# Moving an elementwise product from GpSimd to VectorE, pairing all down-projection blocks and placing two early chains anew, in a fused attention and bilinear-FFN kernel

## Chip, cores, metric

The kernel runs on one core of one Trainium2 chip. The metric is device time in microseconds (us) for one execution. Most executions of one kernel agree within 0.3%. Spans in the profile are 1.4 to 2 us shorter than the times, since they run from the first to the last instruction.

## The reference

Eight batches of eight heads attend to 32 memory slots. The result goes through a feed-forward layer that multiplies two projections.

```python
# q, k, v: (8, 8, 576, 64); phi: (8, 8, 576, 32)
a = softmax(phi, over the sequence)                 # written out in the reference
k_m = einsum('bhsm,bhsd->bhmd', a, k)
v_m = einsum('bhsm,bhsd->bhmd', a, v)
attn = softmax(q @ k_m^T / sqrt(64), over the 32 slots)
x = (attn @ v_m) as (4608, 512)                     # tokens x (heads * head_dim)
out = ((x @ w_a) * (x @ w_b)) @ w_out               # w_a, w_b: (512, 1536), w_out: (1536, 512)
```

## The kernel before

`attn @ v_m @ w_a` is computed as `attn @ (v_m @ w_a)`. So each batch has a **chain** (sums of k and v, transposes, scores, exponentials E, denominators, reciprocals R, the product A = E·R) and a **fold** of the weights (`vab`). They feed the **up-projections** (`pa`, `pb`, giving `ht`) and the **down-projections**. The chain of batch b+1 is cut into units that are laid, slot by slot, between the up-projections of batch b. An up-projection of 288 tokens takes two slots here. Some of the code, cuts marked:

```python
        def normalise(g, hfs=slice(0, 2)):                       # two per batch: g = 0, 1
            ...
            nc.scalar.activation(out=t["R", g][:, sl], in_=t["L", g][:, sl], func=AF.Exp, scale=-1.0)
            engine = nc.vector if b < 3 else nc.gpsimd           # <- the product of E and R
            engine.tensor_tensor(out=attn[b][:, g, sl], in0=t["E"][:, g, sl], in1=t["R", g][:, sl], op=ALU.mult)
```

The down-projections of two blocks of 128 tokens are done as one pair with seven products of half blocks in place of eight. That needs four sums of `ht` blocks per pair, on GpSimd. The second needs the first and the third needs the second. The fourth needs neither.

```python
    def sum_tokens(cidx, engine):
        ...
        for out, in0, in1, op in ((t[0], a21, a22, ALU.add), (t[1], t[0], a11, ALU.subtract),
                                  (t[2], a12, t[1], ALU.subtract), (t[3], a11, a21, ALU.subtract)):
            engine.tensor_tensor(out=out, in0=in0, in1=in1, op=op)
            yield
```

Of the 36 blocks, the first four are done early by themselves, thirty in fifteen pairs, block 34 by itself, and block 35 last, in two half-width accumulations (`last_down`).

A PSUM bank holds what the matmuls write until another engine has copied it out; this is called evacuating it. An up-projection evacuates its two banks by ScalarE (`a_sb`) and VectorE (`ht`). All PSUM tiles share eight banks, given out in the order of last use:

```python
        pa = banks.tile([P, HALF], F32, name="pa")
        ...                                                      # two matmuls of 288 columns
        nc.scalar.copy(out=a_sb, in_=pa)
        ...
        pb = banks.tile([P, HALF], F32, name="pb")
        ...                                                      # two matmuls
        nc.vector.tensor_tensor(out=ht[:, i, t0:t0 + HALF], in0=a_sbs[hf - hfs[0]], in1=pb, op=ALU.mult)
```

The order of the units is written as strings, one word per slot (`nr1` is the second product with its reciprocals, `qt` a transpose of q, `kv` and `km` the sums of k and v and their evacuation, a prime the batch after next):

```python
    every = "- sc+e0 e1 den0 v0+x0a+x0b - - nr0 exp0' - v1+x1a x1b+qt0' den1 - exp1' v2+x2a+x2b nr1+qt1' - kv'+km' qt2' kvt'+qt3' L - -"
```

The softmax here doesn't subtract the row's maximum and nothing guards it: scores larger than these inputs give would overflow.

Of the kernel before, what the change touches and what calls it, by code (L numbers as in the profile page):

```python
# [8 lines left out]
F32 = mybir.dt.float32  # L9
F16 = mybir.dt.float16  # L10
AF = mybir.ActivationFunctionType
ALU = mybir.AluOpType

P = 128
CS = 16.0
# [3 lines left out]
def kernel(  # L19
# [167 lines left out]
    def units(b):  # L187
# [129 lines left out]
        def normalise(g, hfs=slice(0, 2)):  # L317
            if g == 0 and hfs.start == 0:
                attn[b] = mid.tile([P, 2, S], F16, name="A")
            sl = slice(HALF * hfs.start, HALF * hfs.stop)  # L320
            if hfs.start == 0:
                t["R", g] = small.tile([P, S], F16, name="R")
            nc.scalar.activation(out=t["R", g][:, sl], in_=t["L", g][:, sl], func=AF.Exp, scale=-1.0)  # L323
            engine = nc.vector if b < 3 else nc.gpsimd
            engine.tensor_tensor(out=attn[b][:, g, sl], in0=t["E"][:, g, sl], in1=t["R", g][:, sl], op=ALU.mult)  # L325

        def fold(lo, hi, zs):
# [73 lines left out]
    def down(cidx):  # L401

        po, bank = banks.take([P, d_model], F32, "po", hold=True)
        yield from down_part(po, bank, cidx, 0, NFF)

    def last_down(cidx):

        pair, c = divmod(cidx, NI)
        w = d_model // 2
        for x in range(2):  # L410
            cs = slice(w * x, w * (x + 1))
            po = banks.tile([P, w], F32, name="pl")
            o_sb = opool.tile([P, w], F32, name="o_sb")
            for i in range(NFF):
                nc.tensor.matmul(po, ht[:, i, P * c:P * (c + 1)], wo_sb[:, i, cs],
                                 start=(i == 0), stop=(i == NFF - 1))
            nc.scalar.mul(out=o_sb[:, :w // 2], in_=po[:, :w // 2], mul=1.0 / (CS * CS))
            nc.vector.tensor_scalar(out=o_sb[:, w // 2:], in0=po[:, w // 2:], scalar1=1.0 / (CS * CS), scalar2=None,
                                    op0=ALU.mult)
            for z, engine in enumerate((nc.sync, nc.scalar)):  # L420
                slot = 2 * c + z
                engine.dma_start(out=out_rows[2 * pair + slot // NI, slot % NI, :, cs],
                                 in_=o_sb[64 * z:64 * z + 64, :])

    EARLY = 4

    def early_downs():
# [28 lines left out]
    def sum_tokens(cidx, engine):  # L456

        h_sums[cidx] = spool.tile([P, 4, KH, P], F16, name="h_sums")
        t = [h_sums[cidx][:, x] for x in range(4)]
        (a11, a12), (a21, a22) = ([tokens_of(cidx + y, x) for x in range(2)] for y in range(2))  # L460
        for out, in0, in1, op in ((t[0], a21, a22, ALU.add), (t[1], t[0], a11, ALU.subtract),
                                  (t[2], a12, t[1], ALU.subtract), (t[3], a11, a21, ALU.subtract)):
            engine.tensor_tensor(out=out, in0=in0, in1=in1, op=op)  # L463
            yield

    def store(o_sb, cidx):
        pair, c = divmod(cidx, NI)
        for z in range(2):
            slot = 2 * c + z
            nc.sync.dma_start(out=out_rows[2 * pair + slot // NI, slot % NI], in_=o_sb[64 * z:64 * z + 64, :])  # L470

    def two_downs(self, cidx):
        S1, S2, S4, S3 = (h_sums[cidx][:, x] for x in range(4))
        T1, T2, T3, T4 = (w_sums[:, x] for x in range(4))
        (a11, a12), (a21, a22) = ([tokens_of(cidx + y, x) for x in range(2)] for y in range(2))
        scale = 1.0 / (CS * CS)

        def products(po, lhs, rhs, first=False):
            for i in range(KH):
                nc.tensor.matmul(po, lhs[:, i], rhs[:, i], start=first and i == 0,  # L480
                                 stop=i == KH - 1, skip_group_check=not first)
                if i < KH - 1:
                    yield

        def part(po, name):
            x = ppool.tile([P, NH], F32, name=name)
            nc.scalar.mul(out=x, in_=po, mul=scale)
            return x

        def plus(o, po, x):  # L490
            nc.vector.scalar_tensor_tensor(out=o, in0=po, scalar=scale, in1=x, op0=ALU.mult, op1=ALU.add)

        o1, o2 = (opool.tile([P, d_model], F32, name="o_sb") for _ in range(2))
        y, ybank = banks.take([P, NH], F32, "py", hold=True)
        yield from products(y, a11, quarter(0, 0), True)
        u1 = part(y, "u1")
        yield
        v, vbank = banks.take([P, NH], F32, "pv", hold=True)
        self.brim = True
        yield from products(v, S1, T1, True)  # L500
        u5 = part(v, "u5")
        yield
        yield from products(y, S2, T2)
        u2 = part(y, "u2")
        yield
        yield from products(v, S4, quarter(1, 1))
        banks.free(vbank)
        plus(o1[:, NH:], v, u2)
        self.brim = False
        yield  # L510
        yield from products(y, S3, T3)
        plus(o2[:, NH:], y, u5)
        yield
        x, xbank = banks.take([P, NH], F32, "px", hold=True)
        self.brim = True
        yield from products(x, a12, quarter(1, 0), True)
        banks.free(xbank)
        plus(o1[:, :NH], x, u1)
        store(o1, cidx)
        self.brim = False  # L520
        yield
        yield from products(y, a22, T4)
        banks.free(ybank)
        nc.scalar.mul(out=o2[:, :NH], in_=y, mul=scale)
        store(o2, cidx + 1)
        yield

    BLOCKS = B // 2 * NI
    LEAD = 24
    PLAIN = 0  # L530
    PAIRED = range(EARLY + PLAIN, BLOCKS - 2, 2)

    class Work:

# [7 lines left out]
            self.next_sum = next(self.sums)  # L542

        def products(self):
            for cidx in range(EARLY, EARLY + PLAIN):
                yield from down(cidx)
            for cidx in PAIRED[:-1]:
                yield from two_downs(self, cidx)
            yield from down(BLOCKS - 2)
            yield from two_downs(self, PAIRED[-1])  # L550

        def add_up(self):
            for n, cidx in enumerate(PAIRED):
                for x in range(4):
                    yield n, NFF * PLAIN + 7 * KH * n + KH * (x + 1)
                    if x == 0:
                        sums = sum_tokens(cidx, nc.gpsimd if n < len(PAIRED) - 1 else nc.vector)
                    next(sums)
            while True:
                yield len(PAIRED), 0  # L560

# [21 lines left out]
        def plan(self, tokens, slots, keep=24):  # L583

            n = min(max(0, tokens // P - PAIRED[0]) // 2, len(PAIRED))
            self.summed = n
            self.ready = NFF * min(PLAIN, tokens // P - EARLY) + 7 * KH * n + NFF * (tokens // P >= BLOCKS - 1)
            self.rate = max(0, self.ready - self.done - keep) / slots
            self.owed = 0.0
            self.sum_ahead()  # L590
# [78 lines left out]
    def chain(b, plan):  # L669


        for x in plan.split():
# [4 lines left out]
            else:  # L677
# [2 lines left out]
    fill(16)  # L680
    chain(0, "exp0 exp1 ks0 f3 kt0 qt0 qt1 f14 s0 e0 ks1 f3 kt1 qt2 qt3 f6 den0 f4 s1 nr0 e1 f6 vs0 vs1 vt0 vt1 den1 f3 "
             "hv0a hx0a nr10 nr11 hv0b hx0b f4")
    ups(steps(0, 0, 4), slots(0, "- hv1a+hx1a - hv1b+hx1b - v1a+x1a - v1b+x1b"))
    load(2)
    ups(steps(0, 4, 12), slots(0, "- - - - v2a+x2a - v2b+x2b"))
    chain(1, "exp0 exp1 y9 ks0 y3 kt0 qt0 qt1 y1 ks1 y3 kt1 s0 e0 qt2 qt3 y6 den0 y2 s1 e1 nr0 y4 den1 y2 vs0 vs1 y1 vt0 vt1 nr1 y1 hv0a hx0a y2 hv0b hx0b y2")
    load(3)
    sum_weights()
    ups(steps(1, 0, 4), slots(1, "y1 hv1a+hx1a hv1b+hx1b y1 v1a+x1a v1b+x1b y3 y3"))
    ups(half_steps(1, 0, 4), slots(1, "- v2a+x2a+v2b+x2b+qt0' - exp0' - exp1'+qt1' - qt2'+kv'+km'+y9"))  # L690
    work.plan(S + HALF, 10)
    ups(half_steps(1, 1, 4), slots(2, "qt3 kvt - sc+e0+e1+den0 - nr0+den1+v0+x0a - - x0b+nr1 - v1+x1b+x1a -"))
    second = "v2_+x2a_+exp0 x2b_ - exp1 qt0+kv+km - qt1+kvt+qt2 qt3 sc+e0 - e1+v0+x0a x0b den0+v1+x1a nr0+L x1b+exp0' den1 - nr1+v2+x2a - x2b+exp1' qt0' kv'+qt1' km' - qt2'+kvt'+qt3'"
    every = "- sc+e0 e1 den0 v0+x0a+x0b - - nr0 exp0' - v1+x1a x1b+qt0' den1 - exp1' v2+x2a+x2b nr1+qt1' - kv'+km' qt2' kvt'+qt3' L - -"
    last = "sc+e0 - e1 - v0 x0b den1+x0a - den0 - nr0+v1+x1a nr1 x1b - - - - - - v2+x2a - - - x2b"
    for b in range(2, B):
        if b == 2:
            load(4)
# [4 lines left out]
            ups(half_steps(b, hf), side[NFF * hf:NFF * (hf + 1)] if hf == 0 else side[NFF:])  # L703
    work.plan(S * B, 1, 0)
    work.pull(work.ready - work.done)
    last_down(B // 2 * NI - 1)
# [1 line left out]
_INS = ['q', 'k', 'v', 'phi', 'moe_w_a', 'moe_w_b', 'moe_w_out']  # L708
_OUTS = [((4608, 512), 'float32')]
# [25 lines left out]
```

## Time and profile before

| | before |
|---|---|
| time, median of 3 | 247.81 us (247.73 to 247.85) |
| span of the profiled execution | 246.4 us |
| TensorE busy | 234.4 us, 95% |
| VectorE / ScalarE / GpSimd busy | 68% / 64% / 61% |

What bounds the kernel (TensorE) is shown in the prediction. Two more views of the kernel before matter for what follows. First, three groups of instructions by line. The columns are line, engine, operation, out<-in and count, then busy us and mean ns, then idle time of the engine just before and what ended it.

```profile
L612 PE MATMUL pb<-A,vab 128*128 128x288 f16 x384 | 76.5, 286 | 0.2
L463 POOL TENSOR_TENSOR h_sums<-ht 128x768 f16<-128x768 f16 x28 | 45.9, 1640 | 34.0 <-DVE ht L615 34.0
L325 POOL TENSOR_TENSOR A<-E,R 128x576 f16<-128x576 f16 x10 | 12.8, 1278 | 11.9 <-ACT R L323 11.6
```

Ten products on GpSimd take 1.28 us each, and the second half of each up-projection (`pb`) hardly waits: 0.2 us in 384 matmuls. Second, the timeline of GpSimd around one second product, of the sixth batch (columns: start, duration, engine, line, operation, tiles):

```profile
151.22 1.64 POOL L463 TENSOR_TENSOR h_sums<-ht,h_sums 128x768 f16<-128x768 f16 x1
152.92 1.28 POOL L325 TENSOR_TENSOR A<-E,R 128x576 f16<-128x576 f16 x1
154.15 1.64 POOL L463 TENSOR_TENSOR h_sums<-ht 128x768 f16<-128x768 f16 x1
```

GpSimd takes the third sum of a pair, then the product, then the fourth sum, without a pause. In the fourth, fifth and seventh batch, too, the second product stands between these two sums (at 100.60, 122.92 and 178.26).

### The profile page before, as it was taken

How to read it: one execution, taken by the hardware profiler on the slowest of the kernel's cores; microseconds unless marked ns; L12 is line 12 of the kernel's file. 1: busy time of each engine (PE TensorE's matmuls, PEld its weight loads, DVE VectorE, ACT ScalarE, POOL GpSimd, SP SyncE). 2: the span in 40 equal slices, each digit the busy share in tenths (PEclk: the TensorE clock that was granted, in tenths of full speed). 3: DMA queues.
4: the chain of work that ended last, by engine and by line, in shares of the span. 5: the costliest groups of instructions: out<-in, count | busy, mean ns of one | idle time of the engine just before them, and what ended most of it. 6: DMA issues, size and time to landing. Idle time of an engine off the chain costs nothing.

```text
span 246.4 us, 7681 instructions
## 1 busy us (share of the span) xinstructions
PE 234.4 (95%) x3049; PEld 167.1 (68%) x3049; DVE 166.5 (68%) x401; ACT 157.9 (64%) x409; POOL 151.1 (61%) x123
## 2 busy tenths in 40 slices
PE   7589999999998999999999999999999999999993
PEld 3354574456655857777787777877787787888782
DVE  3636794477959967876994649865995686756620
ACT  2247772578697489578856768588855877565330
POOL 8724233499799029892899759892849186936000
PEclk9999999999999999999999999999999999999999
DMA  6999999999979804973159732695120303033145
GB/s 198 210 198 206 211 252 207 255 220 271 233 183 207 160 4 108 238 127 85 33 149 208 174 85 45 167 207 145 32 56 3 88 7 82 10 78 71 43 104 128
DMA packets 26036, 33.82 MB, mean 137 GB/s; under 512 B 1936, under 2 KB 20368, under 8 KB 26000
## 3 DMA queue, kind: packets, MB, share of 16 engines
q0 software_dynamic: 19280, 22.71, 50.3%
q1 hardware_dynamic: 6288, 9.90, 16.3%
q10 hardware_dynamic: 432, 0.72, 0.8%
q8 instruction: 24, 0.39, 0.6%
q14 instruction: 12, 0.10, 0.1%
HBM read 42.47 MB, written 9.44 MB: 211 GB/s over the span
## 4 chain that ended last, share of the span: by engine, by line
PE 74%; DMA 17%; DVE 3%; POOL 2%; ACT 1%; issue 1%; ACTq 0%; DVEq 0%; POOLq 0%
PE pa L602 18%; PE pb L612 16%; PE py L480 15%; PE pv L480 8%; DMA phi_sb<-in_phi_dram 6%; DMA wo_sb<-in_moe_w_out_dram 6%; DMA wb_sb<-in_moe_w_b_dram 5%; PE pva L337 5%; PE px L480 4%; PE po L389 3%; PE pkv L213 2%; PE pD L314 1%; PE pscore L292 1%; PE pT L242 1%; POOL q_sb L90 1%
## 5 line engine op out<-in xcount | busy, mean ns | idle before, releaser
L615 DVE TENSOR_TENSOR ht<-a_sb,pb 128x288 f16<-128x288 f16 x192 | 82.9, 448 | 40.2 <-ACT a_sb L605 29.3
L605 ACT CAST a_sb<-pa 128x288 f16<-128x288 f32 x192 | 74.7, 405 | 31.6 <-PE pa L602 31.0
L602 PE MATMUL pa<-A,vab 128*128 128x288 f16 x384 | 76.5, 287 | 1.4 <-DVE A L325 1.4
L612 PE MATMUL pb<-A,vab 128*128 128x288 f16 x384 | 76.5, 286 | 0.2
L463 POOL TENSOR_TENSOR h_sums<-ht 128x768 f16<-128x768 f16 x28 | 45.9, 1640 | 34.0 <-DVE ht L615 34.0
L612 PEld LDWEIGHTS <-vab 128*128 128x128 f16 x384 | 37.0, 98 | 13.2 <-issue 1.9
L602 PEld LDWEIGHTS <-vab 128*128 128x128 f16 x384 | 34.5, 98 | 15.9 <-issue 9.1
L480 PEld LDWEIGHTS <-h_sums 128*128 128x128 f16 x360 | 35.1, 98 | 6.5 <-issue 0.4
L349 ACT CAST vab<-pva 128x512 f16<-128x512 f32 (+1 forms) x52 | 28.1, 558 | 10.0 <-PE pva L337 10.0
L349 DVE CAST vab<-pva 128x512 f16<-128x512 f32 (+1 forms) x52 | 32.8, 643 | 2.4 <-PE pva L337 2.0
L480 PEld LDWEIGHTS <-ht 128*128 128x128 f16 x270 | 26.4, 98 | 5.4 <-issue 0.2
L480 PE MATMUL py<-w_sums,h_sums 128*128 128x256 f16 x180 | 28.5, 272 | 0.0
L463 POOL TENSOR_TENSOR h_sums<-h_sums,ht 128x768 f16<-128x768 f16 x14 | 23.1, 1650 | 1.0
L463 POOL TENSOR_TENSOR h_sums<-ht,h_sums 128x768 f16<-128x768 f16 x14 | 23.0, 1642 | 1.0
L305 ACT ACTIVATE E<-pscore 128x288 f16<-128x288 f32 x32 | 11.4, 416 | 13.6 <-PE pscore L292 13.5
L325 POOL TENSOR_TENSOR A<-E,R 128x576 f16<-128x576 f16 x10 | 12.8, 1278 | 11.9 <-ACT R L323 11.6
L389 PE MATMUL po<-wo_sb,ht 128*128 128x512 f16 x60 | 16.0, 381 | 0.1
L480 PE MATMUL py<-wo_sb,ht 128*128 128x256 f16 x90 | 15.2, 273 | 0.0
L480 PE MATMUL pv<-w_sums,h_sums 128*128 128x256 f16 x90 | 15.2, 273 | 0.0
L204 DVE STREAM_TRANSPOSE qT<-q_sb 128x288 f32<-128x288 f32 x32 | 14.5, 463 | 0.6 <-DMA q_sb<-in_q_dram 0.6
L480 PE MATMUL py<-w_sums,ht 128*128 128x256 f16 x90 | 14.7, 272 | 0.1
L315 ACT ACTIVATE L<-pD 128x288 f32<-128x288 f32 x32 | 11.4, 413 | 5.0 <-PE pD L314 4.8
(66 smaller groups left out, 273.1 us busy)
## 6 DMA issues: line engine op xcount, KB each, us to landing
out_dram<-o_sb SPq DMA_DIRECT2D x70, 128.0 KB, 2.4
kv_sb<-in_v_dram POOLq DMA_DIRECT2D x7, 576.0 KB, 10.5
phi_sb<-in_phi_dram POOLq DMA_DIRECT2D x7, 576.0 KB, 4.6
kv_sb<-in_k_dram POOLq DMA_DIRECT2D x7, 576.0 KB, 8.2
q_sb<-in_q_dram POOLq DMA_DIRECT2D x6, 576.0 KB, 12.8
wo_sb<-in_moe_w_out_dram POOLq DMA_DIRECT2D x3, 512.0 KB, 17.4
q_sb<-in_q_dram POOLq DMA_DIRECT2D x4, 288.0 KB, 12.7
wa_sb<-in_moe_w_a_dram POOLq DMA_DIRECT2D x2, 512.0 KB, 14.8
```

The lines of the kernel that those rows point to most:

```text
L204: nc.vector.transpose(out=t["qT"][:, hp, :].bitcast(F32), in_=qs[b][:, hp, :].bitcast(F32))
L305: nc.scalar.activation(out=Ev[:, g, :, z, :], in_=pss, func=AF.Exp, scale=1.0 / (8.0 * CS))
L325: engine.tensor_tensor(out=attn[b][:, g, sl], in0=t["E"][:, g, sl], in1=t["R", g][:, sl], op=ALU.mult)
L337: nc.tensor.matmul(t["pva", lo, z][g][0][32 * j:32 * j + 32, 0:hi - lo], t["kvT"][64 * r:64 * r + 64, 4 + g, M * j:M * j + M], w_sbs[z][64 ...
L349: engine_copy(out=vabs[b][z][:, g, lo:hi], in_=pva[:, 0:hi - lo])
L389: nc.tensor.matmul(po, ht[:, i, P * c:P * (c + 1)], wo_sb[:, i, :], start=(i == 0), stop=(i == NFF - 1))
L463: engine.tensor_tensor(out=out, in0=in0, in1=in1, op=op)
L480: nc.tensor.matmul(po, lhs[:, i], rhs[:, i], start=first and i == 0, stop=i == KH - 1, skip_group_check=not first)
L602: nc.tensor.matmul(pa, vab[0][:, g, fs], A[:, g, HALF * hf:HALF * (hf + 1)], start=(g == 0), stop=(g == 1))
L605: nc.scalar.copy(out=a_sb, in_=pa)
L612: nc.tensor.matmul(pb, vab[1][:, g, fs], A[:, g, HALF * hf:HALF * (hf + 1)], start=(g == 0), stop=(g == 1))
L615: nc.vector.tensor_tensor(out=ht[:, i, t0:t0 + HALF], in0=a_sbs[hf - hfs[0]], in1=pb, op=ALU.mult)
```

## The change

By the diff, its intent is to take work off GpSimd, whose product takes 2.8 times as long as VectorE's (1.28 and 0.46 us), to do the last two blocks as a sixteenth pair, and to place units where TensorE waits less. The core of the diff, cuts marked:

```diff
-            engine = nc.vector if b < 3 else nc.gpsimd
+            engine = nc.vector
 ...
-    def last_down(cidx):
-        ...
-    def store(o_sb, cidx):
+    def store(o_sb, cidx, cs=slice(0, d_model), engines=(nc.sync, nc.sync)):
 ...                                  # the last pair stores its second block in two halves
-    PAIRED = range(EARLY + PLAIN, BLOCKS - 2, 2)
+    PAIRED = range(EARLY, BLOCKS, 2)
 ...
-                        sums = sum_tokens(cidx, nc.gpsimd if n < len(PAIRED) - 1 else nc.vector)
+                        sums = sum_tokens(cidx, nc.gpsimd if n < len(PAIRED) - 2 else nc.vector)
 ...                                  # first batch's folds, second batch's chain: five more lines
-    ups(steps(0, 0, 4), slots(0, "- hv1a+hx1a - hv1b+hx1b - v1a+x1a - v1b+x1b"))
+    ups(steps(0, 0, 4), slots(0, "hv1a+hv1b hx1b+hx1a - - - v1a+x1a v1b x1b"))
 ...                                  # later batches: second, every, last
-    every = "- sc+e0 e1 den0 v0+x0a+x0b - - nr0 exp0' - v1+x1a x1b+qt0' den1 - exp1' v2+x2a+x2b nr1+qt1' - kv'+km' qt2' kvt'+qt3' L - -"
+    every = "- sc+e0 e1 den0 v0+x0a+x0b - - nr0+exp0' - - v1+x1a qt0' x1b+den1 exp1' - v2+x2a+x2b nr1+qt1' kv'+km' qt2' - qt3' - kvt'+L -"
```

More of the change, by code (lines that the diff above doesn't have):

```diff
@@ L404, in down @@
         yield from down_part(po, bank, cidx, 0, NFF)
-    def last_down(cidx):
-        pair, c = divmod(cidx, NI)
-        w = d_model // 2
-        for x in range(2):
-            cs = slice(w * x, w * (x + 1))
-            po = banks.tile([P, w], F32, name="pl")
-            o_sb = opool.tile([P, w], F32, name="o_sb")
-            for i in range(NFF):
-                nc.tensor.matmul(po, ht[:, i, P * c:P * (c + 1)], wo_sb[:, i, cs],
-                                 start=(i == 0), stop=(i == NFF - 1))
-            nc.scalar.mul(out=o_sb[:, :w // 2], in_=po[:, :w // 2], mul=1.0 / (CS * CS))
-            nc.vector.tensor_scalar(out=o_sb[:, w // 2:], in0=po[:, w // 2:], scalar1=1.0 / (CS * CS), scalar2=None,
-                                    op0=ALU.mult)
-            for z, engine in enumerate((nc.sync, nc.scalar)):
-                slot = 2 * c + z
-                engine.dma_start(out=out_rows[2 * pair + slot // NI, slot % NI, :, cs],
-                                 in_=o_sb[64 * z:64 * z + 64, :])
     EARLY = 4
@@ L469, in store @@
             slot = 2 * c + z
-            nc.sync.dma_start(out=out_rows[2 * pair + slot // NI, slot % NI], in_=o_sb[64 * z:64 * z + 64, :])
+            engines[z].dma_start(out=out_rows[2 * pair + slot // NI, slot % NI, :, cs], in_=o_sb[64 * z:64 * z + 64, cs])
     def two_downs(self, cidx):
@@ L476, in two_downs @@
         scale = 1.0 / (CS * CS)
+        ends = cidx == PAIRED[-1]
         def products(po, lhs, rhs, first=False):
@@ L512, in two_downs @@
         plus(o2[:, NH:], y, u5)
+        if ends:
+            store(o2, cidx + 1, slice(NH, d_model))
         yield
@@ L524, in two_downs @@
         nc.scalar.mul(out=o2[:, :NH], in_=y, mul=scale)
-        store(o2, cidx + 1)
+        if ends:
+            store(o2, cidx + 1, slice(0, NH), (nc.sync, nc.scalar))
+        else:
+            store(o2, cidx + 1)
         yield
@@ L529 @@
     LEAD = 24
-    PLAIN = 0
-    PAIRED = range(EARLY + PLAIN, BLOCKS - 2, 2)
+    PAIRED = range(EARLY, BLOCKS, 2)
     class Work:
@@ L544, in products @@
         def products(self):
-            for cidx in range(EARLY, EARLY + PLAIN):
-                yield from down(cidx)
-            for cidx in PAIRED[:-1]:
+            for cidx in PAIRED:
                 yield from two_downs(self, cidx)
-            yield from down(BLOCKS - 2)
-            yield from two_downs(self, PAIRED[-1])
         def add_up(self):
@@ L554, in add_up @@
                 for x in range(4):
-                    yield n, NFF * PLAIN + 7 * KH * n + KH * (x + 1)
+                    yield n, 7 * KH * n + KH * (x + 1)
                     if x == 0:
-                        sums = sum_tokens(cidx, nc.gpsimd if n < len(PAIRED) - 1 else nc.vector)
+                        sums = sum_tokens(cidx, nc.gpsimd if n < len(PAIRED) - 2 else nc.vector)
                     next(sums)
@@ L586, in plan @@
             self.summed = n
-            self.ready = NFF * min(PLAIN, tokens // P - EARLY) + 7 * KH * n + NFF * (tokens // P >= BLOCKS - 1)
+            self.ready = 7 * KH * n
             self.rate = max(0, self.ready - self.done - keep) / slots
@@ L682 @@
              "hv0a hx0a nr10 nr11 hv0b hx0b f4")
-    ups(steps(0, 0, 4), slots(0, "- hv1a+hx1a - hv1b+hx1b - v1a+x1a - v1b+x1b"))
+    ups(steps(0, 0, 4), slots(0, "hv1a+hv1b hx1b+hx1a - - - v1a+x1a v1b x1b"))
     load(2)
-    ups(steps(0, 4, 12), slots(0, "- - - - v2a+x2a - v2b+x2b"))
-    chain(1, "exp0 exp1 y9 ks0 y3 kt0 qt0 qt1 y1 ks1 y3 kt1 s0 e0 qt2 qt3 y6 den0 y2 s1 e1 nr0 y4 den1 y2 vs0 vs1 y1 vt0 vt1 nr1 y1 hv0a hx0a y2 hv0b hx0b y2")
+    ups(steps(0, 4, 12), slots(0, "- - - - v2a+x2a+v2b+x2b - -"))
+    chain(1, "exp0 exp1 y9 ks0 y3 kt0 qt0 qt1 y1 y3 ks1 qt2 s0 e0 y6 kt1 qt3 den0 y3 s1 nr0 e1 y4 y2 den1 vs0 vs1 vt0 y1 vt1 nr1 hv0a hx0a hv0b y3 hx0b y2")
     load(3)
     sum_weights()
-    ups(steps(1, 0, 4), slots(1, "y1 hv1a+hx1a hv1b+hx1b y1 v1a+x1a v1b+x1b y3 y3"))
-    ups(half_steps(1, 0, 4), slots(1, "- v2a+x2a+v2b+x2b+qt0' - exp0' - exp1'+qt1' - qt2'+kv'+km'+y9"))
+    ups(steps(1, 0, 4), slots(1, "- hv1a+hx1a hv1b+hx1b+y1 - v1a+x1a y3+v1b x1b y3"))
+    ups(half_steps(1, 0, 4), slots(1, "- v2a+x2a+v2b+x2b+qt0' - - qt1'+exp0'+qt2' exp1' - kv'+km'+y9"))
     work.plan(S + HALF, 10)
-    ups(half_steps(1, 1, 4), slots(2, "qt3 kvt - sc+e0+e1+den0 - nr0+den1+v0+x0a - - x0b+nr1 - v1+x1b+x1a -"))
-    second = "v2_+x2a_+exp0 x2b_ - exp1 qt0+kv+km - qt1+kvt+qt2 qt3 sc+e0 - e1+v0+x0a x0b den0+v1+x1a nr0+L x1b+exp0' den1 - nr1+v2+x2a - x2b+exp1' qt0' kv'+qt1' km' - qt2'+kvt'+qt3'"
-    every = "- sc+e0 e1 den0 v0+x0a+x0b - - nr0 exp0' - v1+x1a x1b+qt0' den1 - exp1' v2+x2a+x2b nr1+qt1' - kv'+km' qt2' kvt'+qt3' L - -"
-    last = "sc+e0 - e1 - v0 x0b den1+x0a - den0 - nr0+v1+x1a nr1 x1b - - - - - - v2+x2a - - - x2b"
+    ups(half_steps(1, 1, 4), slots(2, "- kvt qt3 sc+e0+e1+den0 - nr0+den1+v0+x0a - - x0b+nr1 - v1+x1b x1a"))
+    second = "v2_+x2a_+exp0 x2b_ exp1 - qt0+kv+km - qt1+qt2 kvt+qt3 sc+e0 - e1+v0+x0a den0+x0b v1+x1a nr0+L x1b+exp0' den1 - nr1+v2+x2a - x2b+exp1' - qt0'+kv'+qt1' km' - qt2'+kvt'+qt3'"
+    every = "- sc+e0 e1 den0 v0+x0a+x0b - - nr0+exp0' - - v1+x1a qt0' x1b+den1 exp1' - v2+x2a+x2b nr1+qt1' kv'+km' qt2' - qt3' - kvt'+L -"
+    last = "sc+e0 - e1 - v0+x0b - x0a den1 - - den0 v1+x1b x1a+nr0 - - - - nr1+v2+x2a - - - - - x2b"
     for b in range(2, B):
@@ L705 @@
     work.pull(work.ready - work.done)
-    last_down(B // 2 * NI - 1)
 _INS = ['q', 'k', 'v', 'phi', 'moe_w_a', 'moe_w_b', 'moe_w_out']
```

## The prediction

> **What bounds the kernel now.** I read the page first (busy shares, slices, chain), then the busy table in stretches of 4 us, then the timeline where that table shows idle time, then the landing times of the loads.
>
> ```profile
> PE 234.4 (95%) x3049; PEld 167.1 (68%) x3049; DVE 166.5 (68%) x401; ACT 157.9 (64%) x409; POOL 151.1 (61%) x123
> PE   7589999999998999999999999999999999999993
> PE 74%; DMA 17%; DVE 3%; POOL 2%; ACT 1%; issue 1%; ACTq 0%; DVEq 0%; POOLq 0%
> ```
>
> TensorE is busy in 95% of the span and the chain of waits lies on it for 74%; the only other large share is DMA, 17%. The row of slices says where TensorE is not full: the first three or four slices (6.16 us each) and the last. The table by stretches gives the idle time in numbers (columns: stretch, its mean, busy us of PE, PEld, DVE, ACT, POOL, clock, DMA share, GB/s):
>
> ```profile
> 28.00:32.00 4.00, 3.97 (x42) 2.50 (x42) 3.12 (x9) 2.89 (x9) 1.43 (x2) 1.00 1.21 258
> 64.00:68.00 4.00, 3.66 (x61) 2.72 (x60) 3.51 (x11) 2.90 (x8) 3.84 (x3) 1.00 1.21 211
> 68.00:72.00 4.00, 3.76 (x40) 2.48 (x40) 1.88 (x4) 4.00 (x13) 4.00 (x5) 1.00 0.62 125
> 72.00:76.00 4.00, 2.99 (x44) 1.76 (x43) 3.81 (x6) 3.31 (x8) 3.65 (x4) 1.00 1.06 250
> 100.00:104.00 4.00, 3.63 (x97) 2.66 (x82) 3.87 (x12) 1.79 (x6) 3.47 (x3) 1.00 1.17 246
> 148.00:152.00 4.00, 4.00 (x47) 2.87 (x45) 3.70 (x10) 3.33 (x10) 3.84 (x3) 1.00 0.01 4
> ```
>
> From 28 us on, idle TensorE is 0.03 (28 to 32) + 0.14 (48 to 52) + 0.04 (60 to 64) + 0.34 + 0.24 + 1.01 (64 to 76) + 0.08 (88 to 92) + 0.37 (100 to 104) + 0.06 (228 to 232) = 2.3 us. From 104 to 228 us every stretch reads 4.00. There TensorE is the bound, and neither VectorE nor GpSimd ends any wait of it. The DMA share is 1.2 until 68 us: the early part runs beside a saturated stream of loads. The landing times that matter: last third of the second weight 30.55 us, second k 37.34, second half of the second q 42.77, last third of the output weight 48.38, third q 58.96.
>
> **What the Trainium skill says.** "TensorE: Matmul & The Clock Gate", Part 1, gives a warm start-to-start time of N / 2.4 GHz + 2.5 ns: 122, 109 and 216 ns for 288, 256 and 512 columns. The chain of waits agrees: four `pa` of 288 columns in 0.49 us, three `py` of 256 in 0.33 us. The means of 273 to 287 ns in the groups are latencies that overlap, and "Perfetto Trace Analysis", Identifying the Most-Contended Engine, says the same of matmul busy time; so I count with the start-to-start times. "SBUF — State Buffer", SBUF: two separate sides, says that a VectorE op with two SBUF inputs and a GpSimd op that reads SBUF take one port pair by turns, the whole instruction long. The trace shows it once, for just the operation that moves here, the product of E with the reciprocals:
>
> ```profile
> 70.65 0.46 DVE L325 TENSOR_TENSOR A<-E,R 128x576 f16<-128x576 f16 x1
> ...
> 73.17 1.64 POOL L463 TENSOR_TENSOR h_sums<-ht 128x768 f16<-128x768 f16 x1 [0.27 <-DVE ht L615]
> ...
> 73.70 1.42 DVE L325 TENSOR_TENSOR A<-E,R 128x576 f16<-128x576 f16 x1
> 74.89 1.73 POOL L463 TENSOR_TENSOR h_sums<-h_sums,ht 128x768 f16<-128x768 f16 x1
> 75.17 0.28 PE L602 MATMUL pa<-A,vab 128*128 128x288 f16 x1 [1.01 <-DVE A L325]
> ```
>
> With GpSimd on its loads the product took 0.46 us; under a block sum it took 1.42 us, and TensorE waited 1.01 us for it. "GPSIMD Engine Reference", Performance versus the Vector engine, puts a two-input add on GpSimd at 1.96 times VectorE (fp32); here the same f16 product takes 1.28 us on GpSimd, 2.8 times 0.46.
>
> **Part 1, blocks 34 and 35 as a pair.** Removed: 12 matmuls of 512 columns (block 34) and 24 of 256 (block 35): 12 x 0.216 + 24 x 0.109 = 5.21 us. Added: one pair, 42 x 0.109 = 4.58 us. All of it lies behind the last up-projection, where TensorE has no other work: **-0.63 us** on the path. Against it stand three small costs of the tail. (a) The block sums of the last pairs run on VectorE (0.55 us each, four per pair), now eight, not four. Before, block 34's 2.6 us of matmuls hid half of them; the one place where a sum stood between two evacuations cost TensorE 0.23 us (0.06 of it idle, the rest under the latency of the matmul before) at 231 us. Two such places now: +0.25. (b) The last evacuation is 256 columns on ScalarE alone (0.39 us) and not two halves side by side (0.28, 0.29): +0.1. (c) The sync queue:
>
> ```profile
> 239.34 3.20 SPq L470 DMA_DIRECT2D out_dram<-o_sb  x4
> 242.54 0.29 DVE L418 TENSOR_SCALAR o_sb<-pl 128x128 f32<-128x128 f32 x1 [1.01 <-ACT o_sb L417]
> 242.64 1.19 SPq L422 DMA_DIRECT2D out_dram<-o_sb  x2
> ```
>
> Some 0.55 us per issue; in the kernel before, the last store (issued at 243.28) already stands 0.45 us behind its data (242.83). After, the two full-width stores of block 34 become ready about 0.3 us before the last matmul ends and take 1.1 us, so the last store again stands behind them, by 0.5 to 0.9 us: +0.1. Part 1 in sum: -0.63 + 0.45 = **-0.2 us**.
>
> **Part 2, the first batch's folds and the second batch's chain placed anew.** The order of TensorE's instructions has 106 changes between full and tiled matmuls, before 114: four fewer in the first batch's up-projections, four fewer in the second batch's chain, none after that. One change costs about 0.09 us: three `py` that start at 149.99 end their slots at 150.32, the fold starts at 150.41. 8 x 0.095 = -0.76 us if nothing else binds. But all eight lie before 50 us, beside the loads. The two last folds are now issued together where the first alone stood (30.02 us), and the second needs a weight that lands at 30.55; the chain needs q at 42.77, and its 33rd early down matmul needs the weight of 48.38 (in the kernel before, TensorE takes it up at 48.43). Whoever arrives earlier waits longer. I keep the one early down matmul more that now lies ahead of that point (0.2 us) and a little of the rest: **-0.3 us**.
>
> **Part 3, units moved by a slot in later batches, and the product on VectorE.** Ten products leave GpSimd (12.8 us of 151) and ten come to VectorE: 10 x 0.46 = 4.6 us, and where a block sum is running up to 1.64 us more each. The sums fill about 60% of GpSimd's time from 80 to 228 us, so an estimate is 0.6 x 0.8 = 0.5 us more on average, 9.6 us in all on an engine that is 68% busy. It also now queues behind ScalarE's R (0.69 us), with the evacuations of the up-projections behind it. TensorE sees nothing of that until its PSUM banks run out: eight banks, two held by a pair, two per step of some 0.82 us, so about 2 us of slack. I put +0.2 us for it. The transposes are placed for that: the kv transpose stands two slots later in every steady batch. For the third batch the last q transpose moves to just before the scores that need it, +0.2; the others move away from the sums of k and v, which helps.
>
> **What I add by choice.** The counted sum is -0.2 - 0.3 + 0.2 + 0.2 = -0.1 us. The many single-slot moves look like the result of trials, not of an idea, and what such trials can win is the 2.3 us of idle TensorE. I credit them a good third of it, -0.9 us. Together -1.0: **246.8 us**.
>
> **Rivals.** (1) VectorE becomes a bound in places: each of ten products held by a block sum, evacuations late, TensorE out of banks. For it: 1.42 us and 1.01 us of waiting at 73.70. Against: that wait was for A itself, needed at once; in later batches A has half a batch of time, and all stretches there read 4.00. If half of the products cost 0.5 us: +2.5 us, 249.5. (2) The loads hide everything before 50 us, and the moves do nothing: about 247.7. (3) The waits at 67 to 76 us vanish and the switches count in full: 1.2 + 0.76 + 0.2 off, 245.6. All idle time after 20 us (2.3, and 0.54 in 20 to 28), the switches and part 1 together are 4.2 us, less than the 4.96 that 2% is. So faster by 2% needs more than everything visible.
>
> **Range and chances.** Rival 2 sets the upper middle, rival 3 the lower; rival 1 the tail above. 245.2 to 248.4 should hold it 8 times in 10. Faster by over 2%: 0.02; within 2%: 0.95; slower by over 2% (above 252.8): 0.03.
>
> **What would show it.** 3055 matmuls; GpSimd at about 138 us busy, VectorE at 171 to 176; products on VectorE with a mean of 0.7 to 1.1 us, the long ones under block sums. Folds of the first batch ending at the landing of the weight (30.6), the first up-projection of the second batch at 49.4 to 49.7. Stretches of 104 to 228 us still at 4.00 (if not: rival 1). From the last up-projection to the end 0.1 to 0.4 us less. I am wrong if idle TensorE after 104 us exceeds 1 us, or if the second batch starts before 49 us.

## The result and the profile after

| | before | after |
|---|---|---|
| time, median | 247.77 us (4 runs, 247.45 to 247.85) | 254.11 us (4 runs, 253.93 to 254.28) |
| ratio | | 1.0258, 95% interval 1.0240 to 1.0276 |
| span of the profiled execution | 246.4 us | 252.2 us |

The change made the kernel 2.6% slower. A ratio is the mean time of one kernel's fast runs over the mean of the other's in the same rounds, so it is not quite the ratio of the medians. The page of the kernel after: engines, the row of slices, and the chain that ended last.

```profile
PE 234.6 (93%) x3055; PEld 166.9 (66%) x3055; DVE 179.4 (71%) x416; ACT 158.4 (63%) x410; POOL 138.8 (55%) x113
PE   8689899999989998999989999899989999999992
PE 75%; DMA 11%; issue 4%; DVE 4%; ACT 3%; POOL 1%; DVEq 0%; POOLq 0%
```

TensorE is busy for as long as before (234.6 us against 234.4), in a span 5.8 us longer. From the twentieth slice to the last but one, all nines before, its row now has three eights. No other engine is above 71%, so the shares alone do not say why. Two groups do:

```profile
L594 PE MATMUL pb<-A,vab 128*128 128x288 f16 x384 | 76.4, 286 | 2.9 <-DVE ht L597 2.1
L325 DVE TENSOR_TENSOR A<-E,R 128x576 f16<-128x576 f16 (+1 forms) x17 | 14.6, 858 | 4.6 <-ACT R L323 3.8
```

`pb` now waits 2.9 us, of which 2.1 us for `ht`, which is VectorE's evacuation of an earlier `pb`: TensorE is out of banks. The product takes 858 ns on average. The mean hides a spread: of 17, two of half the size take 0.31 us, eight about 0.46, two 0.67 and 0.97, and five 1.47 to 1.91 us. The table by stretches (as in the prediction) tells where TensorE idles:

```profile
96.00:100.00 4.00, 3.03 (x37) 2.06 (x38) 3.33 (x6) 3.79 (x9) 3.92 (x3) 1.00 1.16 184
124.00:128.00 4.00, 3.26 (x90) 2.22 (x79) 3.89 (x9) 1.94 (x7) 4.00 (x5) 1.00 0.65 129
...
156.00:160.00 4.00, 2.74 (x50) 1.72 (x31) 3.93 (x10) 1.53 (x5) 4.00 (x5) 1.00 0.68 141
184.00:188.00 4.00, 2.79 (x24) 1.85 (x22) 3.93 (x13) 1.46 (x4) 0.00 (x0) 1.00 0.30 67
```

In all four, TensorE read 4.00 before. Now it idles 0.7 to 1.3 us in each, while VectorE reads 3.9 in three of them: an engine that is 71% busy on average is full just there. (In the first, at 96 us, VectorE also stood idle for 0.67 us, waiting for R.) The timeline of all engines in the third of these stretches shows one event from cause to effect:

```profile
153.87 1.65 POOL L444 TENSOR_TENSOR h_sums<-ht,h_sums 128x768 f16<-128x768 f16 x1
...
154.78 0.71 ACT L323 ACTIVATE R<-L 128x576 f16<-128x576 f32 x1
...
155.47 1.65 POOL L444 TENSOR_TENSOR h_sums<-ht 128x768 f16<-128x768 f16 x1
155.52 1.91 DVE L325 TENSOR_TENSOR A<-E,R 128x576 f16<-128x576 f16 x1
...
157.35 0.47 DVE L204 STREAM_TRANSPOSE qT<-q_sb 128x288 f32<-128x288 f32 x1
157.75 0.41 DVE L597 TENSOR_TENSOR ht<-a_sb,pb 128x288 f16<-128x288 f16 x1
158.21 0.41 PE L594 MATMUL pb<-A,vab 128*128 128x288 f16 x2 [0.74 <-DVE ht L597]
...
159.12 0.74 DVE L233 TENSOR_SCALAR rep<-pkv,rphi 128x256 f16<-128x256 f32 x2
```

This is the place of the GpSimd timeline shown before. With the product gone from between the third and the fourth sum, the fourth sum moves up to follow the third at once (155.47), and R is ready at 155.49. So the product starts on VectorE at 155.52, in the same instant as the fourth sum, and takes 1.91 us. It ends 0.3 us after the sum. Behind it stand the transpose and the evacuation `ht` that frees the bank for `pb`, so TensorE waits. The products at 124.04 and 182.41 meet a fourth sum in the same way; the one at 97.02 meets a third sum.

From one TensorE start to the next, less what the number of columns takes at the pace of the undisturbed stretches, the lost time of the large waits after 90 us is:

| second product (start, duration) | TensorE waits after it |
|---|---|
| 97.02, 1.59 us | 1.14 us at 98.0 |
| 124.04, 1.85 us | 0.85 at 125.7 and 0.69 at 127.7 |
| 155.52, 1.91 us | 0.91 at 157.2 and 0.69 at 159.2 |
| 182.41, 1.85 us | 0.85 at 184.1 and 0.69 at 186.0 |

Their sum is 5.8 us. The two times of a stall differ from the bracket (0.74 above) since the bracket counts from the modelled end of the matmul before. The second wait of each row ends with `rep`, the evacuation of the sums of k and v (159.12 in the timeline), on VectorE behind the same delay.

### The profile page after: what moved, and what is told of

Its sections match the earlier page's. It is cut to its first block, busy times and chain, and to the rows that moved or that the text cites. A ratio compares the mean times of both kernels' runs of the same rounds, so it can differ in the third digit from the quotient of the medians.

```text
span 252.2 us, 7695 instructions
## 1 busy us (share of the span) xinstructions
PE 234.6 (93%) x3055; PEld 166.9 (66%) x3055; DVE 179.4 (71%) x416; ACT 158.4 (63%) x410; POOL 138.8 (55%) x113
## 3 DMA queue, kind: packets, MB, share of 16 engines
q0 software_dynamic: 19280, 22.71, 49.4%
## 4 chain that ended last, share of the span: by engine, by line
PE 75%; DMA 11%; issue 4%; DVE 4%; ACT 3%; POOL 1%; DVEq 0%; POOLq 0%
PE pa L584 17%; PE pb L594 17%; PE py L462 15%; PE pv L462 8%; DMA wb_sb<-in_moe_w_b_dram 6%; PE pva L337 5%; PE po L389 4%; DMA kv_sb<-in_v_dram 4%; PE px L462 4%; PE pD L314 1%; PE pscore L292 1%; PE pkv L213 1%; ACT a_sb L587 1%; DVE ht L597 1%; DVE rep L233 1%
## 5 line engine op out<-in xcount | busy, mean ns | idle before, releaser
L462 PEld LDWEIGHTS <-h_sums 128*128 128x128 f16 x384 | 37.2, 98 | 9.2 <-issue 2.8
L462 PEld LDWEIGHTS <-ht 128*128 128x128 f16 x288 | 28.1, 98 | 5.7 <-issue 0.4
L462 PE MATMUL py<-w_sums,h_sums 128*128 128x256 f16 x192 | 30.3, 272 | 0.0
L325 DVE TENSOR_TENSOR A<-E,R 128x576 f16<-128x576 f16 (+1 forms) x17 | 14.6, 858 | 4.6 <-ACT R L323 3.8
L462 PE MATMUL pv<-w_sums,h_sums 128*128 128x256 f16 x96 | 16.0, 272 | 1.6 <-DVE rep L233 1.6
L469 ACT ACTIVATE u<-py 128x256 f32<-128x256 f32 x32 | 12.4, 387 | 7.8 <-PE py L462 7.6
L462 PE MATMUL py<-wo_sb,ht 128*128 128x256 f16 x96 | 16.0, 273 | 0.0
L462 PE MATMUL py<-w_sums,ht 128*128 128x256 f16 x96 | 15.5, 272 | 0.1
L462 PE MATMUL px<-wo_sb,ht 128*128 128x256 f16 x96 | 15.4, 273 | 0.0
## 6 DMA issues: line engine op xcount, KB each, us to landing
wa_sb<-in_moe_w_a_dram POOLq DMA_DIRECT2D x2, 512.0 KB, 15.1
```

The source lines that it names most:

```text
L462: nc.tensor.matmul(po, lhs[:, i], rhs[:, i], start=first and i == 0, stop=i == KH - 1, skip_group_check=not first)
L469: nc.scalar.mul(out=x, in_=po, mul=scale)
```

## The experiments

Three theories stood at the start. **L, the lock**: the product on VectorE is held for the whole length of a GpSimd block sum, VectorE's order holds the evacuations behind it, and TensorE runs out of banks. **P, placement**: it is the moved units that put too much VectorE work in one place, whoever does the product. **T, the tail**: the sixteenth pair costs more than it saves. All kernels are correct except the one that says so. A few executions were slower than their fellows by over 1.5% and are left out of the ratios.

### Which part of the change carries it

The first four runs were on one chip, and each run below is compared with the kernel before on its own chip. **after_gp** is the kernel after with the product of the later batches on GpSimd again:

```diff
-            engine = nc.vector
+            engine = nc.vector if b < 3 else nc.gpsimd
```

> The changed kernel with one line restored: from the fourth batch on the product of E with the reciprocals is on GpSimd again; pairs and all moved units stay. Theory L (port lock: the second product of a batch is held by a block sum for 1.6 to 1.9 us, the evacuations behind it come late, TensorE runs out of PSUM banks): the waits at 98, 125 to 128, 157 to 159 and 184 to 186 us (1.1 + 1.5 + 1.6 + 1.5 = 5.8 us) go, time 247.8 to 248.6 us. Rival S (the moved units, above all the sums of k and v one slot earlier, make the waits): they stay, 253 to 254 us. Rival P (pairs at the end): 253 to 254 us, with the loss behind the last up-projection.

Measured: 247.70 us (before 247.94), ratio 0.9985 [0.9975, 0.9995]. The whole loss is gone. Its stretch from 156 us (156.0 to 160.0) again reads 4.00, and the timeline of GpSimd there has the old order, the product ahead of the fourth sum:

```profile
152.57 1.28 POOL L325 TENSOR_TENSOR A<-E,R 128x576 f16<-128x576 f16 x1
153.80 1.65 POOL L444 TENSOR_TENSOR h_sums<-ht 128x768 f16<-128x768 f16 x1
```

**before_dve** is the kernel before with that one line of the change alone.

```diff
-            engine = nc.vector if b < 3 else nc.gpsimd
+            engine = nc.vector
```

> The kernel before with that one line alone: product on VectorE for all batches, nothing moved. Theory L: the same 1.6 to 1.9 us products and 3 to 7 us of idle TensorE, 251 to 255 us. Rival S (the engine alone is harmless, the moved units do it): 247 to 248.5 us.

Measured: 253.87 us, ratio 1.0237 [1.0213, 1.0261]. One line makes nearly the whole loss, without any moved unit. P falls as the cause of the loss by itself. The long products are at the same four places, as VectorE's timeline shows for the third:

```profile
155.06 1.89 DVE L325 TENSOR_TENSOR A<-E,R 128x576 f16<-128x576 f16 x1
```

It differs from the kernel after in two things. TensorE waits once per long product (0.77 to 1.28 us), not twice: the second wait of 0.69 us does not occur with the old order of units. And there is a fifth long product, in the last batch: at 203.39 us it starts 0.05 us after a first sum, takes 1.90 us, and TensorE waits 1.17 us. So the two kernels lose about the same in partly different ways: 2.1 of the 5.8 us in the kernel after are second waits, which need the delay and the moved units together.

**pairs_only** is the kernel before with the sixteen pairs and their stores; the strings and the engine of the product stay.

```diff
-    PAIRED = range(EARLY + PLAIN, BLOCKS - 2, 2)
+    PAIRED = range(EARLY, BLOCKS, 2)
 ...                                  # with it last_down out, stores and sums of the last pairs as in the change
```

> The changed kernel with the strings of slots and the product's engine as before: only the pairing of the last two blocks is left. The prediction's part 1: -0.2 us, so 247.6. If its tail costs are larger than I counted (sums on VectorE, store queue), 248 to 248.5. Rival P: 252 or more.

Measured: 248.01 us (before 247.94), ratio 0.9993 [0.9983, 1.0003]. T falls.

**front_only** is the kernel before with only the strings of the first two batches (and of the third batch's chain) from the kernel after, six lines in all:

```diff
-    ups(steps(0, 4, 12), slots(0, "- - - - v2a+x2a - v2b+x2b"))
+    ups(steps(0, 4, 12), slots(0, "- - - - v2a+x2a+v2b+x2b - -"))
 ...                                  # and five more
```

> The kernel before with only the moved units of the first two batches (folds of batch 0, chain of batch 1, slots up to the third batch's chain). The prediction's part 2: -0.3 us with no more than +0.2 for the late q transpose, so 247.5 to 247.8; if all eight mode changes counted, 247.0; if arriving earlier only waits longer for the loads, 247.8 to 248.2.

Measured: 247.96 us, ratio 0.9994 [0.9983, 1.0005]. No gain that can be told from none: eight fewer changes of matmul form before 50 us are worth at most 0.4 us by this interval.

### Is it the lock, and what takes it

SBUF is the on-chip memory in which the operands of both engines lie here. "SBUF — State Buffer", in SBUF: two separate sides, says of the port pair that VectorE and GpSimd share that "whichever … starts first gets the pair for the whole instruction; the other fully blocks", and for a VectorE operation with two SBUF inputs only against a GpSimd operation that reads SBUF. The next runs, all but the last on one chip, test both halves of this.

**after_gate** keeps the product on VectorE but makes GpSimd wait for it: a tiny operation on GpSimd reads four columns of A after each product, so that the next sum cannot start before the product is done.

```diff
             engine.tensor_tensor(out=attn[b][:, g, sl], in0=t["E"][:, g, sl], in1=t["R", g][:, sl], op=ALU.mult)
+            if b > 2:
+                gate = small.tile([P, 4], F16, name="gate")
+                nc.gpsimd.tensor_tensor(out=gate, in0=attn[b][:, g, 0:4], in1=attn[b][:, g, 0:4], op=ALU.add)
```

> The changed kernel, product on VectorE, but GpSimd gets a tiny operation that reads the first four columns of each product from the fourth batch on, so that no block sum that stands behind it in the program's order can start before the product is done. The queue of VectorE is the same as in the changed kernel. Theory L (port lock against the block sum that starts at the same moment): the long products fall from 1.6 to 1.9 us to some 0.46, the waits of TensorE go, 247.3 to 248.3 us. Rival Q (VectorE is late because the product waits for ScalarE's R and then stands in the queue ahead of the evacuations, whatever its length): the waits stay, 252 to 254 us.

Measured: 250.57 us (before 247.87), ratio 1.0102 [1.0086, 1.0117]. Of the loss of 2.6%, 1.6 come back. The gated products near 125, 155 and 181 us take 0.46 us, and TensorE waits no more than 0.2 us at a time there. The forecast of 247.3 to 248.3 us was missed, for one got worse (all engines, around 97 us):

```profile
96.89 0.76 POOL L90 DMA_DIRECT2D q_sb<-in_q_dram  x1
97.22 2.42 DVE L325 TENSOR_TENSOR A<-E,R 128x576 f16<-128x576 f16 x1 [0.68 <-ACT R L323]
97.65 1.67 POOL L447 TENSOR_TENSOR h_sums<-h_sums,ht 128x768 f16<-128x768 f16 x1
```

This gate stands too late in GpSimd's queue: a sum ahead of it began at 97.65. The product ended 0.3 us after that sum, and TensorE waited 1.97 us, most of the 2.5 us of TensorE time that this run still loses against after_gp from 90 to 232 us. Why the product, started 0.43 us before the sum, was held already beside the DMA issue is open: the other products that began beside an issue took at most 0.46 us, some sixty over all traces, but two more of the runs show a longer one there (0.84 us at 70.68 in after_halfsums and at 70.50 in after_chainhalves).

**after_nolock** gives a wrong result on purpose (relative error 0.96). Each block sum on GpSimd computes four columns only, and two fills of the rest take up the time. The fills write SBUF but do not read it.

```diff
-            engine.tensor_tensor(out=out, in0=in0, in1=in1, op=op)
+            if engine is nc.gpsimd:
+                engine.tensor_tensor(out=out[:, :, P - 4:], in0=in0[:, :, P - 4:], in1=in1[:, :, P - 4:], op=op)
+                engine.memset(out[:, :, :P - 4], 0.0)
+                engine.memset(out[:, :, :P - 4], 0.0)
+            else:
+                engine.tensor_tensor(out=out, in0=in0, in1=in1, op=op)
```

> Wrong result on purpose: the changed kernel, in which each block sum on GpSimd becomes a 4-column sum (it keeps the wait for ht) and two fills of the other columns, which read nothing from SBUF. If only an operation that reads SBUF on both sides locks: products at 0.46 us, 247 to 248.5 us. If writing alone locks as well: products still 1.0 to 1.9 us and 250 to 254 us. Rival Q: 252 to 254 us with short products.

Measured: 247.64 us, ratio 0.9980 [0.9971, 0.9989]. Two fills of 0.72 us and a short sum of 0.24 us are about as long as the sum they stand for (1.65). Yet the products take 0.45 to 0.51 us, also this one, which starts 0.02 us after a fill (all engines):

```profile
151.76 0.72 POOL L446 MEMSET h_sums<- 128x744 f16 x1
151.78 0.46 DVE L325 TENSOR_TENSOR A<-E,R 128x576 f16<-128x576 f16 x1
```

So it is neither how long GpSimd is busy nor VectorE's load. L holds, and the page's condition, that the GpSimd operation must **read** SBUF, agrees with this case: 0.46 us beside a fill, which only writes, up to 1.9 us beside a sum, which reads. These two kinds of operation are the only ones tried.

**after_halfsums** cuts each GpSimd sum into two of half the size, one behind the other. If the pair is held for one instruction, the product should get in after half a sum.

```diff
+            if engine is nc.gpsimd:
+                for h in (slice(0, KH // 2), slice(KH // 2, KH)):
+                    engine.tensor_tensor(out=out[:, h], in0=in0[:, h], in1=in1[:, h], op=op)
 ...                                  # the sums on VectorE as before
```

> The changed kernel with each block sum on GpSimd in two operations of half the columns (about 0.85 us each). Theory L with the lock held for one instruction and VectorE next in line: the long products fall to 0.5 to 1.3 us, the waits of TensorE to less than a third, 248 to 249.5 us. If GpSimd keeps the pair over both halves, nothing changes: 253.5 to 254.5 us.

Measured: 259.17 us, ratio 1.0453 [1.0427, 1.0480]. Neither forecast (248 to 249.5, or 253.5 to 254.5 us) came true: it got slower than the kernel after. All engines, from 72 us:

```profile
72.67 1.81 POOL L446 TENSOR_TENSOR h_sums<-ht 128x384 f16<-128x384 f16 x2
...
73.74 6.23 DVE L325 TENSOR_TENSOR A<-E,R 128x576 f16<-128x576 f16 x1
74.42 1.78 POOL L446 TENSOR_TENSOR h_sums<-h_sums,ht 128x384 f16<-128x384 f16 x2
...
77.88 1.76 POOL L446 TENSOR_TENSOR h_sums<-ht 128x384 f16<-128x384 f16 x2
80.02 0.40 PE L588 MATMUL pa<-A,vab 128*128 128x288 f16 x1 [5.67 <-DVE A L325]
```

The product waits 6.23 us, through seven half sums, and ends 0.3 us after the last. At six boundaries between two half sums GpSimd kept the pair. With the halves side by side, each half sum is independent of the one just before it (it needs the half before last), so GpSimd has the next one ready: it begins without a pause. The two other long products of this run, of 2.85 and 2.05 us, passed three more such boundaries in vain.

**after_chainhalves** keeps the halves but orders them so that most of them need the one just before: the first halves of sums one to three in a row, then the second halves of one and two, of three, then both of four.

```diff
+            order = (((0, h0), (1, h0), (2, h0)), ((0, h1), (1, h1)), ((2, h1),), ((3, h0), (3, h1)))
 ...                                  # the loop over this order, and the sums on VectorE as before
```

> The changed kernel with each block sum in two halves as in the run with half sums (that one made the product at 73.7 us last 6.23 us, over seven half sums that followed each other without a gap), but in an order in which most halves wait for the one just before, which leaves a gap of some 0.06 to 0.08 us between them. Theory G (VectorE gets the port only where GpSimd has nothing ready to run): the product at 73 us falls to 0.6 to 1.5 us, no product over 2.4 us, and the time lies below the half sums' 259.2 us by 5 us or more, 249.5 to 253.5 us. Rival (the number of GpSimd's operations or their size decides): products of 3 to 6 us again, 257 to 260 us.

Measured: 249.35 us (before 247.96), ratio 1.0044 [1.0025, 1.0064]. The product that took 6.23 us (VectorE's timeline):

```profile
73.56 1.18 DVE L325 TENSOR_TENSOR A<-E,R 128x576 f16<-128x576 f16 x1
```

GpSimd's half sums there run from 73.52 to 74.42 and from 74.50. In the pause of 0.08 us, in which the later one waits for the result of the earlier, VectorE got the pair. No product in this run is longer than 1.18 us. The same additions in the same halves cost 259.2 or 249.4 us, by their order alone (which also moves them in time, so that all five second products after 90 us now meet no sum).

Counted over all fourteen traces, for products held by a sum: at a boundary between two sums **with** that pause VectorE got in 14 times of 14. Without a pause it got in 8 times of 17: 5 of 5 between whole sums, 3 of 12 between halves. So readiness alone, the theory put on record for this run, does not decide it; what does is open. In the kernel after, no product was held beyond the one sum it met. Its three worst (124.04, 155.52, 182.41) are as long as they are because they began about 0.1 us or less after that sum's start.

### How much slack TensorE has

**gp_hold** is after_gp (product on GpSimd, no lock) with VectorE held by seven fills at the place of each second product.

```diff
+            if b > 2 and g == 1:
+                for _ in range(7):
+                    nc.vector.memset(warm, 0.0)
```

> The changed kernel with the product on GpSimd again, and in place of the second product of each batch from the fourth on VectorE fills a spare tile seven times (7 x 0.27 = 1.9 us, writes only, no wait for R). It measures the second half of the theory by itself: VectorE away for 1.9 us at that place. Theory L: TensorE waits as in the changed kernel, 4 to 6 us in sum, 252 to 254 us. If the lock hurts in another way than by making VectorE late: 247.5 to 249 us.

Measured: 257.35 us (before 247.87), ratio 1.0396 [1.0357, 1.0434]. The dose came out larger than planned, and so did the time (252 to 254 us were expected): each fill took the planned 0.27 us, but 0.39 us passed from the start of one to the start of the next, 0.12 us of it between the two (VectorE's part of the timeline):

```profile
155.90 2.62 DVE L328 MEMSET warm<- 128x256 uint32 x7
```

TensorE waits 1.45 us at 157.67 and 0.69 us at 160.24, and the same at 125.6 and 185.1; 1.44 us at 97.6 and at 212.2. So any delay of VectorE does it, without a lock, and the two doses give the slack, counted from the end of VectorE's operation before: 2.62 - 1.45 = 1.17 us here (the first fill follows at once), and in the kernel after, where 0.12 us lie between `ht` and the product, 0.12 + 1.91 - 0.91 = 1.12 us and 0.12 + 1.85 - 0.85 = 1.12 us. The product at 97.02 gives 1.12 us as well, 0.67 + 1.59 - 1.14, when the 0.67 us that VectorE stood idle for R are counted: there the wait for R took up over half of the slack. VectorE may be kept from its evacuations for 1.1 to 1.2 us at these places before TensorE waits. The second wait is 0.69 us for either dose: once the first stall occurs, it comes on top.

### A version that beats both

One collision is old: the second product of the third batch ran on VectorE in the kernel before, and is in the prediction as the only sight of the lock. **gp_gate** is after_gp with one gate for it, so that GpSimd's sums start after that product.

```diff
             load(4)
+            gate = small.tile([P, 4], F16, name="gate")
+            nc.gpsimd.tensor_tensor(out=gate, in0=attn[2][:, 1, 0:4], in1=attn[2][:, 1, 0:4], op=ALU.add)
```

> A version that should beat both: the changed kernel with the product on GpSimd from the fourth batch on, and one tiny GpSimd operation that reads the third batch's second product after the loads of the fifth batch, so that the next pair's first block sum starts after that product and not 0.8 us before it needs the port. Theory L: that product falls from 1.47 to 0.46 us, the wait of 1.23 us at 73 us to about 0.2, so 246.5 to 247.0 us. If GpSimd's sums are late for TensorE after the gate, or the wait has another cause: 247.5 us or more.

Measured: 246.69 us (before 247.78), ratio 0.9944 [0.9929, 0.9959]: 1.1 us under the kernel before by the medians and 7 us under the kernel after. All engines:

```profile
73.38 0.46 DVE L325 TENSOR_TENSOR A<-E,R 128x576 f16<-128x576 f16 x1
...
73.92 0.20 POOL L682 TENSOR_TENSOR gate<-A 128x4 f16<-128x4 f16 x1 [1.06 <-DVE A L325]
74.08 1.63 POOL L444 TENSOR_TENSOR h_sums<-ht 128x768 f16<-128x768 f16 x1
```

The product is back at 0.46 us, the sums start 1.3 us later than they would (72.80 in after_gp), and TensorE's wait at this place falls from 1.22 to 0.22 us.

**before_gate** is the kernel before with the same gate.

> The kernel before with that gate alone. Theory L: the product at 73.7 us falls from 1.42 to 0.46 us and the wait of TensorE from 1.18 to 0.2 us, so about 1.0 us less than the kernel before, 246.8 us. Otherwise 247.5 to 248.

Measured: 246.99 us, ratio 0.9962 [0.9948, 0.9976]. So 0.9 us of the gain is the gate's own. What is left, 0.4 us by the ratios, would be the pairs' and moved units' (after_gp alone has 0.9985), but the two intervals overlap.

**split_gate** is gp_gate with the first product of each batch on VectorE and only the second on GpSimd.

```diff
+            engine = nc.vector if b < 3 or g == 0 else nc.gpsimd
```

> As the version that should beat both, but the first product of each batch is on VectorE and the second on GpSimd. In the changed kernel the first products met no sum (0.45 to 0.67 us, the last batch 0.97), the second ones did. Theory L: the place, not the engine's load, decides, so no new wait of TensorE: within 0.3 us of the version with both on GpSimd. If it is VectorE's load or its queue behind R that hurts: 1 to 3 us more.

Measured: 247.04 us, ratio 0.9968 [0.9952, 0.9983], 0.35 us above gp_gate by the medians, a little more than the 0.3 us expected. No new wait of 0.3 us or more appears, so there is no sign of the 1 to 3 us of the rival. Moving the product where it does no harm gains nothing either: GpSimd was not what TensorE waited for.

## Why the prediction was wrong

Predicted 246.8 us, 245.2 to 248.4; measured 254.11 us. The chance given to "slower by over 2%" was 0.03.

**What bounds the kernel.** Right: TensorE, and 3055 matmuls in the kernel after as counted.

**Part 1, the pair (predicted -0.2 us).** Not contradicted, and not shown: pairs_only has 0.9993, about -0.2 us of 248, with an interval that includes zero. In its trace the stretch from the last up-projection to the end is not shorter, as it should be, but 0.1 us longer (17.58 us, before 17.46).

**Part 2, the early chains (predicted -0.3 us).** Not contradicted: front_only has 0.9994, about -0.15 us, and again zero is inside. Rival 2, that the loads hide it, cannot be told from it. (The three matmuls at 149.99 us that this part calls `py` are `px` in the trace; its 0.09 us per change stands.)

**Part 3, the product on VectorE: the step that failed.** It reads: "TensorE sees nothing of that until its PSUM banks run out: eight banks, two held by a pair, two per step of some 0.82 us, so about 2 us of slack. I put +0.2 us for it." The term measured about +6 us (lost TensorE time by start times from 90 to 232 us: 21.1 us in the kernel after, 15.1 in after_gp; the spans are 252.2 and 245.9 us). The sum of VectorE's extra work was close: ten products cost it 14.6 - 3.9 = 10.7 us more than the seven it has in after_gp, against the 9.6 us estimated. What failed is what was made of that sum, in two ways.

- The collisions were taken as chance, 0.6 × 0.8 us each. They are not chance. In four batches the product used to stand between the third and the fourth sum on GpSimd. Its removal closes that gap, and in three of the four the fourth sum then starts about 0.1 us or less before the product, which waits for the whole of it. A mean delay of 0.5 us would lie within the slack at these three places and cost nothing; products of 1.85 and 1.91 us do not.
- The slack was counted from the banks as 2 us. gp_hold and the kernel after measure 1.1 to 1.2 us. VectorE works strictly in order, as "TensorE: Matmul & The Clock Gate", Part 1, states of its queue. The timeline agrees: `ht` at 157.75 waits behind the product and a transpose that TensorE did not need yet, though the copy that it needs (`a_sb`) had ended by 157.08 at the latest. Once the slack is used up, the second wait of 0.69 us comes on top, which the prediction did not have either.

**The credit of -0.9 us "by choice".** Unfounded: all moves and pairs together, without the product, measure 0.9985 (-0.4 us). Had the idle time at 73 us been looked at for its cause, which the prediction itself shows, one gate would have been the way to win it.

**The rivals.** Rival 1 named the mechanism: VectorE a bound in places, evacuations late, TensorE out of banks. Its size, 249.5 us, was too small: it took half of ten products at 0.5 us, where four events cost 1.1 to 1.6 us each. Its counterargument, that "A has half a batch of time", failed since it is not A that is needed: it is what VectorE has queued behind A.

**The checks.** GpSimd 138.8 us (predicted about 138) and products with a mean of 0.86 us (0.7 to 1.1) came as predicted; VectorE has 179.4 us, above 171 to 176. "Stretches of 104 to 228 us still at 4.00 (if not: rival 1)" was the check that told: 3.26, 3.52, 2.74 and 2.79. Idle TensorE from 104 to 228 us by the same table is 4.05 us, where "exceeds 1 us" was named as the sign of being wrong. Two smaller ones failed as well: the first up-projection of the second batch starts at 49.78 us (49.4 to 49.7), and the end after the last up-projection is 0.1 us longer (0.1 to 0.4 less).

## What to carry to other kernels

Before moving an operation from one engine to another, look at what the freed slot will be filled with and whether that collides with the operation in its new place; a mean over the stage does not tell this. Where, as here, VectorE reads two SBUF operands and GpSimd reads SBUF, order the two by a dependence (a tiny gate) or leave both on GpSimd, even at 2.8 times the duration, if GpSimd is off the path. Judge slack by the in-order queue behind the delayed operation, count the wait for its input with it, and measure it by holding the engine for a known time.

## What the Trainium skill lacked or had wrong

- "SBUF — State Buffer", SBUF: two separate sides: the page says who holds the pair, but not who gets it next. Here VectorE got it in 14 of 14 cases when GpSimd's next sum came after a pause of 0.08 us, and in 8 of 17 when it came without; one product waited 6.23 us through seven half sums.
- The same place: its condition that the GpSimd operation must read SBUF agrees with these runs (fills of 0.72 us left the product at 0.46 us). The page does not say that a held product ends 0.3 us after the sum that held it.
- "GPSIMD Engine Reference", Performance versus the Vector engine: it gives 1.96 times for an fp32 add; for the f16 product here it is 2.8 times (1.28 and 0.46 us), for the f16 block sum 3.0 times (1.64 and 0.55 us).
- No page that was read for this case tells how to count TensorE's slack from PSUM banks when one in-order engine frees them: counted from banks 2 us, measured 1.1 to 1.2 us.
